# Late queries first in a fused attention and MLP kernel: the order of eight groups, the list's weights and its durations are changed

## The chip, the cores and the metric

The kernel runs on one core of a Trainium2 chip. The metric is device time in microseconds; the kernel before took 809.48 us (median of 3 runs, 809.31 to 809.81). The core's engines each have their own instruction stream: TensorE (PE) multiplies matrices and transposes, VectorE (DVE), ScalarE (ACT) and GpSimd (POOL) work on elements, and SyncE (SP) issues the transfers.

## The reference

```python
scores = (1 / np.sqrt(D)) * q @ k.T           # batch 4, heads 8, seq 576, head_dim 64
scores = np.where(block_i >= block_j, scores, -1e9)    # causal by blocks of 64
attn = softmax(scores) @ v                     # -> x: 2304 tokens x 512

h  = x @ w_in                                  # 512 -> 1024
s  = h * softmax(h)
x  = layernorm(s) * g_ln @ w_out               # 1024 -> 512

h  = x @ w2_in                                 # 512 -> 2048
out = (h * np.cos(h)) @ w2_out                 # 2048 -> 512
```

Three stages follow each other: attention, a first MLP with a layer norm, a second MLP with a cosine.

## The kernel before

Attention is cut into 32 pairs: 4 batches, 4 pairs of heads, and two sets of queries. Early queries are 0 to 255 of a sequence (they see at most 256 keys), late ones 256 to 575 (they see up to 576). A *group* is one batch with one set, so it holds four pairs; there are 8 groups. For each pair `trace_unit` makes score products of 128 queries (L495, the mask by small matmuls L498; the last 64 late queries in L530), the negated maximum (L506, L533 on DVE), the exponential with its sum (L509, L539 on ACT), the normalisation of `e` (L520, L522 or L524 on ACT, DVE or POOL; L551, L553, L555 for the last queries), and transposes of `e` (L581) that are copied to `eT` (L331 on ACT, L327 on DVE). `trace_pv` then multiplies by the values (L606) and leaves the result as high and low parts in `XS`, a ring of 640 tokens. An early pair has 6 transposes, a late one 19.

The groups fill 18 tiles of 128 tokens. When a tile is full, `trace_l1` multiplies it by w_in (L678, 6 matmuls per piece of weight: three products of high and low parts), takes the maximum (L682, DVE), the exponential (L683, ACT), h times softmax (L685, DVE) and the statistics (L694, ACT, and small ones); `trace_lnT` transposes the tile (L711), `trace_l2` multiplies by w_out (L732) and writes rows of yD. The second MLP runs after that (L771, the cosine L782 to L794, L811, L834).

The weights arrive as 64-bit numbers and are split in `trace_weight`: ACT does L635 and L636, DVE L637 and L639, POOL L641, and the high and low parts follow on whichever engine is chosen (L331, L327, L333; L336). w_in has 8 such pieces; the conversion runs while the first groups of attention run.

All this is an order written by a list scheduler at the time the kernel is built (`Scheduler.run`, L146 to L288). Each operation has a duration for every engine that may do it, a priority, and its dependencies. When an engine is free in the scheduler's model, it takes the ready operation with the lowest priority number, less an engine's offset; an operation that several engines can do goes to the one that would end it first by the durations times the `weight` of the engine. For PE an operation that changes the kind of work at a cost may be passed over for one that does not, within `stick`. Priorities come from a table `P` and from intervals per group (L842 to L859): `att_iv` gives each group a start and a length, 10000 ns for an early and 28600 for a late group plus 11000 per ready tile, and 25000 for the first group. The names in `P` shift these: `lead0` to `lead7` per group, `tile` per tile, `w_in` and `w_out` the weights. SP's transfers are ordered by the same list. Where the model has PE idle before 70 us, filler matmuls are put in (L953).

Of the kernel before, what the change touches and what calls it, by code (L numbers as in the profile page):

```python
# [28 lines left out]


P = {
    "stick": 16439.7,
    "tile": [-12965.7, -74277.3, -6661.5, 1158.2, 10885.7, -12920.0, 6417.0, -10505.1, -20606.0, 50938.7, -9661.6, 11449.5, 1147.6, 46246.4, -28708.3, -23619.0, -6397.2, -18072.8],
    "pair": [-2458.3, -5103.1, -897.3, 2369.0],
    "weight": {"p": 1.0, "s": 1.58, "v": 3.08, "g": 2.909, "q": 1.0},
    "att_slope": -0.012,
    "att_pe": 59777.9,
    "att_vec": 21108.6,
    "mlp_pe": -40513.6,
    "mlp_vec": 11906.3,  # L40
    "w_in": 4918.0,
    "w_out": 54908.8,
    "w_out_step": 3502.4,
    "w2_direct": -41386.8,
    "w2_step": 13014.7,
    "lead0": -7523.6,
    "lead1": 5369.7,
    "lead2": 14753.4,
    "lead3": 15930.2,
    "lead4": 14060.0,  # L50
    "lead5": -4515.5,
    "lead6": 10595.0,
    "lead7": -69178.6,
    "l2": 10939.5,
    "l2_step": 22673.5,
    "prep": -11366.2,
}


# [12 lines left out]
class Scheduler:  # L72
# [24 lines left out]
    def op(self, engs, fn, r=(), w=(), prio=0.0, port=False, iss=0.0, kind="M"):  # L97


        o = Op()  # L100
        o.engs, o.fn, o.prio, o.port, o.iss, o.kind = engs, fn, prio, port, iss, kind
        o.idx, o.succ, o.pred, o.ready, o.start = len(self.ops), [], [], {}, None
        deps, tiles = set(), []
        for k in list(r) + list(w):
            t = k[0] if isinstance(k, tuple) else k
            if isinstance(t, Lt) and t not in tiles:
                tiles.append(t)
        for k in r:
            if k in self.last_w:
                deps.add(self.last_w[k])  # L110
        for k in w:
            if k in self.last_w:
                deps.add(self.last_w[k])
            deps.update(self.reads.get(k, ()))
        for k in r:
            self.reads.setdefault(k, []).append(o)
        for k in w:
            self.last_w[k] = o
            self.reads[k] = []
        deps.discard(o)  # L120
        o.ndep = len(deps)
        for d in deps:
            d.succ.append(o)
        for t in tiles:
            t.refs += 1
        o.tiles = tiles
        self.ops.append(o)
        return o
# [163 lines left out]
def fused_kernel(ctx: ExitStack, tc: tile.TileContext, qT, kT, vm, vt, w_in, w_out, g_ln, w2_in, w2_out, out):  # L292
# [3 lines left out]
    NB = 4  # L296
# [5 lines left out]
    op = sch.op  # L302
# [115 lines left out]
    MLP = {"xs", "e1", "junk", "LN", "yb"}  # L418


    groups = [(b, g) for g in range(2) for b in range(NB)]
    gp_list = [(gi, p) for gi in range(len(groups)) for p in range(NPAIR)]

    def g_q0(gi):
# [5 lines left out]
    first, first_e = {}, {}  # L430
# [9 lines left out]
    def trace_prep(i, prio):  # L440
        gi, p = gp_list[i]
        b, g = groups[gi]
        pr = b * NPAIR + p
        nq, q0 = g_nq(gi), g_q0(gi)
        nk = q0 + nq
        nj = 2 if g == 0 else 4
        rv = Lt("rv", [128, 5, 2, 64], F32)
        rq, rk = Lt("rq", [128, nq], F32), Lt("rk", [128, nk], F32)
        dma(lambda: rq.ap, lambda: qT[pr, :, q0:q0 + nq], 512 * nq, w=[rq], prio=prio)
        dma(lambda: rk.ap, lambda: kT[pr, :, 0:nk], 512 * nk, w=[rk], prio=prio)  # L450
        dma(lambda: rv.ap[:, 0:nj], lambda: vm[pr, :, 0:nj, :].rearrange("p j (h d) -> p j h d", h=2), 65536 * nj,
            w=[(rv, 0)], prio=prio)
        if g == 1:
            dma(lambda: rv.ap[0:64, 4], lambda: vt[pr].rearrange("p (h d) -> p h d", h=2), 32768, w=[(rv, 1)], prio=prio)
        op({"s": c_s(nq), "v": c_v2(nq), "g": c_g(nq)}, lambda e: copy(e, rq.ap, rq.ap, SCALE), [], [rq], prio, port=True)
        return rq, rk, rv
# [4 lines left out]
    def trace_unit(i, t, prep, eT, prio):  # L461
        gi, p = gp_list[i]
        g = groups[gi][1]
        rq, rk, rv = prep
        q0 = g_q0(gi)
        W = 128 * (t + 1)
        us = Lt("us", [128, 8], F32)
        if g == 0:
            if t == 0:
                first_e[i] = [Lt("e", [128, 2, 128 * x + 128], F32) for x in range(2)]  # L470
            e = first_e[i][t]
        else:
            e = Lt("e", [128, 2, W] if t < 4 else [128, 640], F32)
# [3 lines left out]
        if row:  # L477
# [3 lines left out]
            scl = first[i]  # L481
            scs = [lambda h=h: scl[h].ap[:, 128 * t:128 * t + W] for h in range(2)]
            keys = [(x, t) for x in scl]
        else:
            scl = [Lt("psb", [128, W if t < 4 else 288], F32) for h in range(2)]
            scs = [lambda h=h: scl[h].ap for h in range(2)]
            keys = scl
        if t < 4:
            c0 = 128 * t - q0

            def f_s(spans):

                for n, (c, o, w) in enumerate(spans):
                    for h in range(2):
                        PE.matmul(scl[h].ap[:, o:o + w], lhsT=rq.ap[rows[h], c:c + 128], rhs=rk.ap[rows[h], 0:w], start=(n == 0), stop=False)  # L495
                for n, (c, o, w) in enumerate(spans):
                    for h in range(2):
                        PE.matmul(scl[h].ap[:, o + w - 64:o + w], lhsT=mrow[rows[h], :], rhs=mneg[rows[h], :],  # L498
                                  start=False, stop=(n == len(spans) - 1))
            if row and t == 0:  # L500
                op({"p": 790}, lambda _: f_s(((0, 0, 128), (128, 128, 256))), [rq, rk] + [(x, "a") for x in first_e[i]],
                   [(x, k) for x in scl for k in range(2)], prio, kind="W")
            elif not row:
                op({"p": W / 0.6 + 100}, lambda _: f_s(((c0, 0, W),)), [rq, rk, (e, "a")], scl, prio, kind="W")
            for h in range(2):
                op({"v": c_v(W)}, lambda _, h=h: V.tensor_reduce(out=us.ap[:, h:h + 1], in_=scs[h](), axis=AX.X, op=ALU.max, negate=True),  # L506
                   [keys[h]], [(us, h)], prio)
# [18 lines left out]
        else:  # L526
            for c in range(2):
                def f_s4(_, c=c):
                    for h in range(2):
                        PE.matmul(scl[c].ap[rows[h], :], lhsT=rq.ap[rows[h], 256:320], rhs=rk.ap[rows[h], 288 * c:288 * c + 288], start=True, stop=True)  # L530
                op({"p": 288 / 0.6 + 10}, f_s4, [rq, rk, (e, "a")], [scl[c]], prio, kind="W")
            for c in range(2):
                op({"v": c_v(288)}, lambda _, c=c: V.tensor_reduce(out=us.ap[:, c:c + 1], in_=scl[c].ap, axis=AX.X, op=ALU.max, negate=True),  # L533
                   [scl[c]], [(us, c)], prio)
# [311 lines left out]
    for gi in range(len(groups)):  # L846
        ready = [n for n in range(NT) if n >= done and tile_group[n] < gi]
        done += len(ready)
        ln = (10000.0 if groups[gi][1] == 0 else 28600.0) + T_TILE * len(ready)
        if gi == 0:  # L850
            ln = 25000.0
        att_iv.append((start, ln))
        for k, n in enumerate(ready):
            tile_pr[n] = start + ln * k / len(ready)
        start += ln
# [5 lines left out]
    for i, (gi, p) in enumerate(gp_list):  # L861
        us = (0, 1) if groups[gi][1] == 0 else (2, 3, 4)
        s_, l_ = att_iv[gi]
        pr = s_ + l_ * p / NPAIR - P[f"lead{gi}"] - P["pair"][p]
        prep = trace_prep(i, pr - P["prep"])
        n = 384 if groups[gi][1] == 0 else 1280
        eT = Lt("eT", [128, 2, n], F32)
        for k, t in enumerate(us):
            trace_unit(i, t, prep, eT, pr + l_ / NPAIR * k / len(us))
        trace_pv(i, prep, eT, pr + l_ / NPAIR)  # L870
# [8 lines left out]
    for n in range(NT):  # L879
        pr = tile_pr[n] + P["tile"][n]  # L880
        e = trace_l1(n, pr)
# [18 lines left out]
    for k in range(len(slots) + LAG):  # L900
        if k < len(slots):
            q, c, f = slots[k]
# [6 lines left out]
        if k >= LAG:  # L909
            q, c, f = slots[k - LAG]  # L910
# [20 lines left out]
    with tc.manual_schedule():  # L931
# [9 lines left out]
        for o in order:  # L941
            for t in o.tiles:
                if t.ap is None:
                    make, k, gate, _ = sch.classes[t.cls][t.slot]
# [4 lines left out]
            if o.idle is not None and o.start < WARM:  # L949

                b = singles[o.idle[1].slot] if o.idle[1].cls == "psb" else 2 * o.idle[1].slot
# [35 lines left out]
```

## Time and profile before

| | us |
| --- | --- |
| median of 3 runs | 809.48 |
| the profiled execution's own time | 808.07 |
| its span | 806.3 |
| PE busy in the span | 791.4 |
| DVE, ACT, POOL busy | 598.5, 479.2, 95.0 |

The profiled execution is one run; its span is the part that the trace shows. Busy time is time in which an engine has an instruction in work, and PE also counts as busy when it works slowly or runs fillers. The page's clock row is 9 (90% or more) in all forty slices; finer stretches are read from the rows below.

### The profile page before, as it was taken

How to read it: one execution, taken by the hardware profiler on the slowest of the kernel's cores; microseconds unless marked ns; L12 is line 12 of the kernel's file. 1: busy time of each engine (PE TensorE's matmuls, PEld its weight loads, DVE VectorE, ACT ScalarE, POOL GpSimd, SP SyncE). 2: the span in 40 equal slices, each digit the busy share in tenths (PEclk: the TensorE clock that was granted, in tenths of full speed). 3: DMA queues.
4: the chain of work that ended last, by engine and by line, in shares of the span. 5: the costliest groups of instructions: out<-in, count | busy, mean ns of one | idle time of the engine just before them, and what ended most of it. 6: DMA issues, size and time to landing. Idle time of an engine off the chain costs nothing.

```text
span 806.3 us, 12262 instructions
## 1 busy us (share of the span) xinstructions
PE 791.4 (98%) x4352; PEld 626.7 (78%) x4352; DVE 598.5 (74%) x1335; ACT 479.2 (59%) x1067; POOL 95.0 (12%) x116
## 2 busy tenths in 40 slices
PE   7989999999999999999999999999999999999998
PEld 5667766666776776788888888889988888888996
DVE  5889998667655367579978799866666676767775
ACT  6989998787765466668645667434434333333332
POOL 2222330000000000033322323100000000000000
PEclk9999999999999999999999999999999999999999
DMA  8443553222221101152535744121424022140221
GB/s 277 129 150 100 170 188 101 79 79 89 64 88 64 67 24 68 43 199 73 178 129 172 266 144 156 53 79 60 149 92 163 34 97 87 44 139 27 66 79 39
DMA packets 46029, 86.78 MB, mean 108 GB/s; under 512 B 4240, under 2 KB 18576, under 8 KB 45968
## 3 DMA queue, kind: packets, MB, share of 16 engines
q1 hardware_dynamic: 45968, 86.00, 32.1%
q8 instruction: 34, 0.56, 0.3%
q14 instruction: 27, 0.22, 0.1%
HBM read 67.11 MB, written 18.87 MB: 107 GB/s over the span
## 4 chain that ended last, share of the span: by engine, by line
PE 48%; DVE 1%; DMA 1%; ACT 0%; issue 0%
PE banks L811 24%; PE banks L771 23%; PE banks L732 1%; DMA rw<-w_in 1%; DVE w L336 0%; DVE t L639 0%; DVE ta L792 0%; ACT t L635 0%; DVE tr L787 0%; DVE rw L637 0%; DVE ob L834 0%; DVE LN L336 0%; ACT rw L636 0%; DVE YB L336 0%; ACT w L331 0%
## 5 line engine op out<-in xcount | busy, mean ns | idle before, releaser
L678 PE MATMUL banks<-w,XS 128*128 128x512 f32 x432 | 113.2, 404 | 1.5 <-DVE w L336 0.7
L331 ACT ACTIVATE gt<-ta 128x512 fp32r<-128x512 f32 (+1 forms) x80 | 47.1, 588 | 102.4 <-PE banks L811 69.8
L732 PE MATMUL banks<-LN,w 128*128 128x512 f32 (+1 forms) x480 | 105.6, 373 | 0.8 <-DVE LN L336 0.8
L732 PEld LDWEIGHTS banks<-LN,w 128*128 128x128 f32 x480 | 82.4, 189 | 17.7 <-DVE LN L336 1.2
L678 PEld LDWEIGHTS banks<-w,XS 128*128 128x128 f32 x432 | 77.3, 188 | 21.5 <-issue 4.7
L641 POOL TENSOR_TENSOR t<-t,rw 128x512 uint32<-128x512 uint32 x45 | 68.1, 1519 | 171.2 <-DVE t L639 86.6
L782 ACT ACTIVATE ta<-banks 128x512 f32<-128x512 f32 (+1 forms) x80 | 44.4, 555 | 73.9 <-PE banks L771 71.5
L783 DVE TENSOR_SCALAR ta<-ta 128x512 f32<-128x512 f32 (+1 forms) x80 | 37.0, 463 | 60.2 <-ACT ta L782 60.0
L811 PE MATMUL banks<-wa,gt 128*128 128x512 f32 x324 | 78.8, 390 | 0.0
L811 PE MATMUL banks<-w,gt 128*128 128x512 f32 x324 | 78.7, 390 | 0.0
L509 ACT ACTIVATE e<-banks,us 128x512 f32<-128x512 f32 (+3 forms) x128 | 66.5, 529 | 18.7 <-DVE us L506 17.9
L791 ACT ACTIVATE ta<-tr,hpi 128x512 f32<-128x512 f32 (+1 forms) x80 | 53.9, 674 | 29.0 <-DVE tr L789 28.7
L811 PEld LDWEIGHTS banks<-w,gt 128*128 128x128 f32 x324 | 60.6, 188 | 12.0
L811 PEld LDWEIGHTS banks<-wa,gt 128*128 128x128 f32 x324 | 60.6, 188 | 12.0
L506 DVE TENSOR_REDUCE us<-banks 128x1 f32<-128x512 f32 (+3 forms) x128 | 56.5, 482 | 15.1 <-PE banks L498 13.4
L336 DVE TENSOR_TENSOR gt<-ta,gt 128x512 fp32r<-128x512 f32 (+1 forms) x80 | 52.8, 661 | 14.9 <-ACT gt L331 14.0
L331 ACT ACTIVATE eT<-banks 128x512 f32<-128x512 f32 (+2 forms) x112 | 55.1, 531 | 11.8 <-PE banks L581 10.2
L581 PE MATMUL banks<-ident,e 128*128 128x128 f32 x400 | 58.2, 277 | 3.2 <-ACT e L520 1.8
L792 DVE TENSOR_TENSOR ta<-banks,ta 128x512 f32<-128x512 f32 (+1 forms) x80 | 50.9, 636 | 13.7 <-ACT ta L791 13.4
L581 PEld LDWEIGHTS banks<-ident,e 128*128 128x128 f32 x400 | 46.1, 141 | 16.3 <-ACT e L520 5.9
L606 PE MATMUL banks<-eT,rv 128*64 128x320 f32 (+3 forms) x448 | 53.3, 370 | 0.1
L787 DVE SCALAR_TENSOR_TENSOR tr<-ta,tr 128x512 f32<-128x512 f32 (+1 forms) x80 | 51.7, 646 | 2.2
(121 smaller groups left out, 1389.1 us busy)
## 6 DMA issues: line engine op xcount, KB each, us to landing
rw<-w_out SPq DMA_DIRECT2D x24, 512.0 KB, 4.0
rw<-w_in SPq DMA_DIRECT2D x22, 512.0 KB, 4.1
yD<-YB SPq DMA_DIRECT2D x16, 512.0 KB, 3.0
wa<-yD SPq DMA_DIRECT2D x7, 1024.0 KB, 6.4
rk<-kT SPq DMA_DIRECT2D x16, 288.0 KB, 2.9
oD<-ob SPq DMA_DIRECT2D x18, 256.0 KB, 2.4
w<-yD SPq DMA_DIRECT2D x6, 768.0 KB, 7.1
ob<-oD SPq DMA_DIRECT2D x18, 256.0 KB, 3.3
```

Of the source, the lines that this page charges most:

```text
L331: S.activation(dst, src, AF.Copy, scale=1.0 if scale is None else scale)
L336: (V if eng == "v" else G).tensor_tensor(out=dst, in0=src, in1=h.bitcast(F32), op=ALU.subtract)
L506: op({"v": c_v(W)}, lambda _, h=h: V.tensor_reduce(out=us.ap[:, h:h + 1], in_=scs[h](), axis=AX.X, op=ALU.max, negate=True), [keys[h]], [( ...
L509: op({"s": c_s(W, True, True)}, lambda _, h=h: S.activation(e.ap[:, h, :], scs[h](), AF.Exp, bias=us.ap[:, h:h + 1], scale=1.0, accum_out= ...
L581: PE.transpose(ps.ap[:, 128 * k:128 * k + 128], s(), ident)
L606: PE.matmul(pv.ap[64 * h:64 * h + 64, a:b], lhsT=rv.ap[0:rows, j, h], rhs=eT.ap[0:rows, h, c:c + b - a], start=(n == 0), stop=(n == len(se ...
L641: op({"g": c_g2(512)}, lambda _: G.tensor_tensor(out=t1.ap, in0=t1.ap, in1=lw(), op=ALU.add), [(rw, 0)], [t1], prio)
L678: PE.matmul(h.ap[:, 512 * c:512 * c + 512], lhsT=xs.ap[:, a, kt, :], rhs=w[:, b, 512 * c:512 * c + 512], start=(kt == 0 and a == 0 and b = ...
L732: PE.matmul(y.ap, lhsT=w[:, a], rhs=LN[:, b, kf, s0_:s0_ + len(t), :], start=(kf == 0 and a == 0 and b == 0), stop=(kf == 7 and b == 1))
L771: PE.matmul(ps.ap, lhsT=w[:, a, 128 * kt:128 * kt + 128], rhs=yts[q, c][kt // 2].ap[:, kt % 2, b, :], start=(k == 0), stop=(k == 11))
L791: op({"s": c_s(n, True)}, lambda _: S.activation(cs.ap, r.ap, AF.Sin, bias=hpi, scale=1.0), [r], [cs], prio)
L811: PE.matmul(acc[x][1](), lhsT=gt.ap[:, a, 128 * x:128 * x + 128], rhs=w[:, b, 512:1024], start=(f % 8 == 0 and k == 0), stop=(f % 8 == 7 a ...
```

## The change

The list of groups is turned around: `(1, 0)` puts the four groups of late queries first. Tokens in the ring and rows of yD follow that order. The table `P` has other numbers, among them the weights of ACT ("s", 1.58 to 2.385), DVE ("v", 3.08 to 2.75) and POOL ("g", 2.909 to 1.376). The durations of score products in the list become longer, and the first interval is 38000 when the first group is a late one.

```diff
 P = {
-    "weight": {"p": 1.0, "s": 1.58, "v": 3.08, "g": 2.909, "q": 1.0},
+    "weight": {"p": 1.0, "s": 2.385, "v": 2.75, "g": 1.376, "q": 1.0},
...
-    groups = [(b, g) for g in range(2) for b in range(NB)]
+    groups = [(b, g) for g in (1, 0) for b in range(NB)]
...
-                op({"p": 790}, lambda _: f_s(((0, 0, 128), (128, 128, 256))), [rq, rk] + [(x, "a") for x in first_e[i]],
+                op({"p": 900}, lambda _: f_s(((0, 0, 128), (128, 128, 256))), [rq, rk] + [(x, "a") for x in first_e[i]],
...
-                op({"p": W / 0.6 + 100}, lambda _: f_s(((c0, 0, W),)), [rq, rk, (e, "a")], scl, prio, kind="W")
+                op({"p": W / 0.6 + (120 if W == 384 else 190)}, lambda _: f_s(((c0, 0, W),)), [rq, rk, (e, "a")], scl, prio, kind="W")
...
-                op({"p": 288 / 0.6 + 10}, f_s4, [rq, rk, (e, "a")], [scl[c]], prio, kind="W")
+                op({"p": 288 / 0.6 + 70}, f_s4, [rq, rk, (e, "a")], [scl[c]], prio, kind="W")
...
-            ln = 25000.0
+            ln = 25000.0 if groups[0][1] == 0 else 38000.0
```

What that does to the order is seen on PE and POOL. A name such as `e_253` is one buffer of the program, and `x2` counts equal instructions that follow each other. On PE, at the end of the first wait for loads, the kernel before begins with the first early pairs, in scores of 128 and 256 keys:

```order
L495 MATMUL banks<-rk_109,rq_107 128x128 x2
L495 MATMUL banks<-rk_109,rq_107 128x256 x2
...
L581 MATMUL banks<-ident,e_124 128x128 x2
...
L581 MATMUL banks<-ident,e_125 128x128 x4
L495 MATMUL banks<-rk_120,rq_117 128x128 x2
...
L606 MATMUL banks<-eT_198,rv_111 64x256 x2
```

The changed one begins with two late pairs:

```order
L495 MATMUL banks<-rk_109,rq_107 128x384 x2
...
L495 MATMUL banks<-rk_109,rq_107 128x512 x2
...
L530 MATMUL banks<-rk_109,rq_107 64x288 x2
L495 MATMUL banks<-rk_116,rq_114 128x384 x2
...
L581 MATMUL banks<-ident,e_124 128x128 x3
```

The transposes behind the first scores now belong to a unit of 384 keys, and three tail score products of 288 keys stand where fillers stood. The second place is PE's first layer-1 matmul, L678. Before:

```order
L581 MATMUL banks<-ident,e_254 128x128 x4
L495 MATMUL banks<-rk_187,rq_184 128x128 x2
L495 MATMUL banks<-rk_187,rq_184 128x256 x2
...
L678 MATMUL banks<-w_287,XS 128x512 x6
L606 MATMUL banks<-eT_348,rv_122 64x256 x2
```

After:

```order
L606 MATMUL banks<-eT_422,rv_171 64x64 x2
L581 MATMUL banks<-ident,e_434 128x128 x3
L530 MATMUL banks<-rk_305,rq_302 64x288 x2
L581 MATMUL banks<-ident,e_459 128x128 x8
...
L581 MATMUL banks<-ident,e_468 128x128 x4
L678 MATMUL banks<-w_380,XS 128x512 x6
```

Before, it stands behind the scores of the fourth early pair; now the sixth late pair is under way. The third place is the start of POOL, after the masks are written. Before, it holds only sums of weights (L641):

```order
L938 MEMSET mhalf 128x1
L641 TENSOR_TENSOR t_196<-t_196,rw_113 128x512
L641 TENSOR_TENSOR t_249<-t_249,rw_115 128x512
L641 TENSOR_TENSOR YB<-YB,rw_168 128x512
L641 TENSOR_TENSOR YB<-YB,E_87 128x512
```

After, scalings of queries (L333), normalisations (L524) and parts of the split (L333, L336) stand among them:

```order
L938 MEMSET mhalf 128x1
L333 TENSOR_SCALAR rq_107<-rq_107 128x320
...
L524 TENSOR_SCALAR e_124<-e_124,us_179 128x384
...
L524 TENSOR_SCALAR e_196<-e_196,us_213 128x384 x2
...
L641 TENSOR_TENSOR t_267<-t_267,rw_182 128x512
...
L333 TENSOR_SCALAR w_380<-t_267 128x512
L336 TENSOR_TENSOR w_380<-t_267,w_380 128x512
```

Over the whole program POOL's normalisations (L524 and L555) go from 3 to 100, 30 of them of 384 columns and most of these in the late groups; fillers go from 112 to 51, and the places at which PE goes from one kind of work to another, fillers left out, from 242 to 218.

## Rows read from the trace of the kernel before

**Rows 1.** The page, busy time of each engine.

```profile
PE 791.4 (98%) x4352; PEld 626.7 (78%) x4352; DVE 598.5 (74%) x1335; ACT 479.2 (59%) x1067; POOL 95.0 (12%) x116
```

**Rows 2.** Busy by stretch: us, PE, PEld, DVE, ACT, POOL, clock, DMA share, GB/s.

```profile
5.30:59.50 54.20, 46.73 (x381) 33.61 (x379) 46.36 (x153) 48.01 (x150) 12.78 (x13) 0.97 0.59 191
59.50:112.20 52.70, 52.16 (x333) 38.93 (x332) 51.32 (x143) 50.10 (x138) 18.88 (x25) 1.00 0.43 136
112.20:344.40 232.20, 232.20 (x1453) 160.66 (x1453) 148.53 (x403) 161.56 (x398) 9.91 (x28) 1.00 0.25 78
```

**Rows 3.** Groups, 5.3 to 59.5 us; columns: busy us, mean ns, idle before.

```profile
L678 PE MATMUL banks<-w,XS 128*128 128x512 f32 x55 | 15.9, 416 | 1.5 <-DVE w L336 0.7 <-DVE w L327 0.5 <-DVE E L685 0.3
L581 PE MATMUL banks<-ident,e 128*128 128x128 f32 x54 | 9.8, 287 | 2.6 <-ACT e L520 1.3 <-DVE e L522 1.2
L495 PE MATMUL banks<-rk,rq 64*128 64x256 f32 x40 | 7.9, 410 | 0.0
L606 PE MATMUL banks<-eT,rv 128*64 128x256 f32 x36 | 6.3, 433 | 0.1
```

**Rows 4.** Timeline of PE, early pairs; columns: start us, us, operation.

```profile
24.55 0.87 PE L606 MATMUL banks<-eT,rv 128*64 128x256 f32 x8
25.35 0.93 PE L495 MATMUL banks<-rk,rq 64*128 64x128 f32 x8
...
26.26 1.66 PE L678 MATMUL banks<-w,XS 128*128 128x512 f32 x6
27.76 0.60 PE L581 MATMUL banks<-ident,e 128*128 128x128 f32 x4
```

**Rows 5.** Timeline of PE, late pairs and layer 1.

```profile
142.43 1.94 PE L581 MATMUL banks<-ident,e 128*128 128x128 f32 x16
144.30 2.42 PE L606 MATMUL banks<-eT,rv 128*64 128x320 f32 x20
146.66 0.92 PE L495 MATMUL banks<-rk,rq 64*128 64x384 f32 x4
...
344.36 7.11 PE L678 MATMUL banks<-w,XS 128*128 128x512 f32 x30
351.31 1.98 PE L732 MATMUL banks<-LN,w 128*128 128x512 f32 x8
```

**Rows 6.** Timeline of PE after a wait, and that stretch's busy times.

```profile
38.92 1.65 PE L495 MATMUL banks<-rk,rq 64*128 64x128 f32 x6 [0.80 <-ACT eT L331]
...
40.00:50.00 10.00, 9.14 (x58) 6.04 (x54) 7.72 (x26) 8.79 (x27) 2.59 (x2) 0.88 0.52 171
```

**Rows 7.** Groups of ACT, conversion of weights, whole span.

```profile
L636 ACT ACTIVATE rw<-rw 128x512 uint32<-128x512 uint32 x46 | 31.2, 678 | 3.9 <-DMA rw<-w_in 2.5 <-DMA rw<-w_out 1.3
...
L635 ACT ACTIVATE t<-rw 128x512 f32<-128x512 f32 x45 | 30.1, 672 | 5.1 <-DMA rw<-w_in 1.8 <-DVE w L336 1.5 <-DVE wa L336 0.7
```

**Rows 8.** Groups of a tile's chain behind layer 1.

```profile
L682 DVE TENSOR_REDUCE st<-banks 128x1 f32<-128x1024 f32 x18 | 21.9, 1218 | 10.0 <-PE banks L678 10.0
L685 DVE SCALAR_TENSOR_TENSOR E<-banks,E 128x1024 f32<-128x1024 f32 x18 | 21.9, 1216 | 1.4 <-ACT E L683 1.3
...
L694 ACT ACTIVATE junk<-E,st 128x1024 bf16<-128x1024 f32 x18 | 20.7, 1149 | 3.2 <-DVE st L687 3.2
L683 ACT ACTIVATE E<-banks,st 128x1024 f32<-128x1024 f32 x18 | 20.2, 1123 | 4.6 <-DVE st L682 4.5
```

**Rows 9.** DMA issues: KB each, median us to landing.

```profile
rk<-kT SPq DMA_DIRECT2D x16, 288.0 KB, 2.9
...
rk<-kT SPq DMA_DIRECT2D x16, 128.0 KB, 2.5
```

**Rows 10.** Normalisation on POOL and DVE (group, ns min/median/max), with DVE beside it.

```profile
L524 POOL TENSOR_SCALAR e<-e,us x3: 374/376/943, 59.0 to 68.7; 128x128 f32<-128x128 f32 x3
...
59.40 0.74 DVE L647 SCALAR_TENSOR_TENSOR w<-t,g_sb,w 128x512 fp32r<-128x512 f32 x1
...
L522 DVE TENSOR_SCALAR e<-e,us 128x384 f32<-128x384 f32 x15 | 6.1, 418 | 0.4
```

More of the change, by code (lines that the diff above doesn't have):

```diff
@@ L31 @@
 P = {
-    "stick": 16439.7,
-    "tile": [-12965.7, -74277.3, -6661.5, 1158.2, 10885.7, -12920.0, 6417.0, -10505.1, -20606.0, 50938.7, -9661.6, 11449.5, 1147.6, 46246.4, -28708.3, -23619.0, -6397.2, -18072.8],
-    "pair": [-2458.3, -5103.1, -897.3, 2369.0],
-    "weight": {"p": 1.0, "s": 1.58, "v": 3.08, "g": 2.909, "q": 1.0},
[L36 to L56, printed above, removed]
+    "stick": 24783.0,
+    "tile": [-14359.3, -37985.7, 6113.4, -3055.7, 24465.2, 4623.7, 3526.9, -32896.1, -22525.7, 27230.1, -18199.6, 22478.0, 37632.5, 59648.4, -15097.6, 596.8, -22562.3, -32058.0],
+    "pair": [-10908.6, 3875.9, 1648.0, 792.0],
+    "weight": {"p": 1.0, "s": 2.385, "v": 2.75, "g": 1.376, "q": 1.0},
+    "att_slope": 0.053,
+    "att_pe": 74866.7,
+    "att_vec": 151894.2,
+    "mlp_pe": -14159.9,
+    "mlp_vec": 34158.7,
+    "w_in": -10429.3,
+    "w_out": 307495.7,
+    "w_out_step": 1138.4,
+    "w2_direct": 73027.9,
+    "w2_step": 12920.1,
+    "lead0": 7512.5,
+    "lead1": 22625.7,
+    "lead2": 8969.7,
+    "lead3": -7974.6,
+    "lead4": -9446.8,
+    "lead5": -67400.4,
+    "lead6": -7144.6,
+    "lead7": -13408.6,
+    "l2": 5241.5,
+    "l2_step": 15170.5,
+    "prep": 36287.5,
 }
```

## The prediction

> **What bounds the kernel now.** I began with the page: TensorE (PE) is busy for 791.4 of 806.3 us [rows 1]. By that figure 14.9 us could be won at most, but it also counts the filler matmuls of L953, slowed matmuls and matmuls whose tail merely waits, so I went on to the busy time by stretch [rows 2]. Two stretches show PE full: from 59.5 to 344.4 us it idles 0.54 and 0.00 us. The stretch 5.3 to 59.5, in which the early pairs run beside the conversion of w_in and the first tiles of layer 1, is different: PE 46.73 of 54.20, ACT 48.01, DVE 46.36, PE's clock 0.97. No engine is full; three are nearly full and take turns.
>
> Next I asked what PE computes there. The costliest groups [rows 3] give 55 L678 (9 groups of 6), 54 transposes L581, 40 wide score matmuls (4 in each of 10 score operations) and 36 wide L606 (4 in each of 9 value products). The timeline [rows 4] prices each from start to start where PE does not wait: a value product 25.35 − 24.55 = 0.80; a score operation with its masks 26.26 − 25.35 = 0.91; six L678 27.76 − 26.26 = 1.50; a transpose (144.30 − 142.43)/16 = 0.117 [rows 5]. So the stretch needs 9×0.80 + 10×0.91 + 54×0.117 + 9×1.50 = 7.2 + 9.1 + 6.3 + 13.5 = 36.1 us. It takes 54.2, and 18.1 us are lost. ACT alone accounts for 48.0 − 36.1 = 11.9 of them, as it has 48.0 us to do beside 36.1 of PE; the other 6.2 are hand-offs, in which ACT too is idle. Part of the loss shows as busy time: between 40 and 50 the clock is 0.88, and there six score matmuls took 1.65 where eight take 0.93 [rows 4, 6], after a PE wait of 0.80 for ACT.
>
> In 112.2 to 344.4, where mostly late pairs run, ACT is busy for 161.56 and DVE for 148.53 of 232.20 [rows 2], that is 70% and 64%. Late pairs keep PE full and leave ACT and DVE time.
>
> **The change part by part.** PE computes the same matmuls. What moves is which pairs stand beside the weight conversions.
>
> *Late pairs in the first stretch.* One late pair gives PE 19 transposes at 0.117, 2.2 us, value products of 146.66 − 144.30 = 2.36 [rows 5], and three rounds of score products, each at no less than the early 0.91: at least 7.3 us. In the new order some five pairs' worth stands before the first L678, 36.5 us. ACT needs 0.70 × 36.5 = 25.5 for them. Converting w_in's 8 pieces takes ACT 8 × (0.672 + 0.678) = 10.8 [rows 7]. Together 36.3: ACT's need falls from 11.9 above PE's to none. The hand-offs remain in kind, but each is now followed by pieces of three to eight transposes (0.35 to 0.94) or a 2.36 us product rather than by two to four transposes or 0.80; I keep 70% of the 6.2. Left of the 18.1: 4.3. Bounds: 2 (a third of the hand-offs) and 18.1 (nothing won).
>
> *Early pairs later.* They still want more of ACT than PE takes, but there they stand among layer-1 and layer-2 matmuls of tiles already finished, with w_in and w_out converted. That cover can run out at the turn from late to early groups, where a tile's layer 1 in the new order ends some 7 us of PE work before its next step. The chain that must fit between is L682 1.218, L683 1.123, L685 1.216, L694 1.149 [rows 8], 4.7 us before hand-offs. If three of them and some short operations use the same engines for others meanwhile, it does not fit. Bounds 0 and 12 (ACT's whole excess, met again); I take 1.0, as the stretch 59.5 to 112.2 does much the same with an idle of 0.54 [rows 2].
>
> *First loads.* Keys come as 288 KB in 2.9 us where 128 KB took 2.5 [rows 9]; the first scores are later by 0.4, and a scaling of 320 columns for 256 makes it 0.5. Nothing covers it. Bounds 0.4 and 1.
>
> *Changes of kind on PE.* The order has 24 fewer places at which PE goes from one kind of work to another (218 for 242, fillers aside). Six L678 cost 1.50 from start to start, thirty 351.31 − 344.36 = 6.95 [rows 4, 5]; from 1.50 = a + 6b and 6.95 = a + 30b, one beginning costs a = 0.14. 24 of them are 3.3 us; transposes and value products show less, so I take −2.0. Bounds 0 and −3.3.
>
> *POOL.* Normalisations on POOL (L524, L555) go from 3 to 100, 30 of them 128x384. ACT and DVE are relieved by them; on PE's path they can cost. A pass of 384 on DVE takes 0.418; on POOL only 128 columns are shown, at 0.374, 0.376 and 0.943, the last beside L647 on DVE from 59.40 [rows 10]. So a 384 pass lies between 0.42 (as DVE) and 3 × 0.374 + 0.57 of waiting = 1.69. While PE has other pairs' transposes and products to do, 1.2 us are hidden, and I count 0. If that cover is gone it is up to 1.27 each; the rival below prices it.
>
> *Score durations, fillers, phase 2.* The durations and the first interval only steer the list: 0 by themselves. Fillers fall from 112 to 51; they run when PE would wait, so 0. MLP2 and the tail keep their rows: 0, with no bound other than 0.5 either way.
>
> Sum, against the profiled execution: 806.3 − 18.1 + 4.3 + 1.0 + 0.5 − 2.0 = 792.0 us of span. Its own time lies 808.07 − 806.3 = 1.77 above its span: 793.8. The median of the runs, 809.48, lies 1.41 above that execution: **795.2 us**. The best ends (2, 0, 0.4, −3.3) give 787.3 of span, 790.5.
>
> **Rivals.** *Half the gain.* PE still waits for ACT at the start, since maxima, exponentials and copies of late pairs come in a chain before any other pair is ready, and the turn costs 3 us. With 9.0 of 18.1 left, 3.0, 0.5 and −1.5: 799.2 of span, 802.4 us. For it: DVE is at 46.36 in the stretch now and a late pair brings 64% of its PE time besides. Against: ACT's two conversions are the bigger part and do fit.
>
> *No change.* The 18.1 us belong to the ramp itself, whichever pairs come first: all of it left gives 806.3 + 1.0 + 0.5 − 2.0 = 805.8, or 809.0 us. [...] Against: the two rates of ACT to PE, 48.0 to 36.1 and 161.6 to 232.2.
>
> *POOL on PE's path: slower.* The first 30 passes of 384 sit in the stretch where only two or three pairs are open; each pass delays that half pair's transposes. At 1.2 us, near the upper end since the L524 row with DVE beside it shows the wait, 18 of 30 exposed cost 21.6 us: 817 us. It turns from faster to slower by over 0.2% at (811.1 − 795.2)/1.2 = 13 passes. For it: 0.943 against 0.374. Against: in the new first stretch PE has other work in reach, and ACT and DVE lose just these passes. The row, then, shows a POOL pass that took two and a half times as long with a DVE instruction beside it. The Trainium skill, "SBUF — State Buffer", Who interferes with whom, has the two engines share one pair of ports as an exclusive lock, the loser fully blocked; "Perfetto Trace Analysis", Optimizing Scalar/DVE Operations, adds that moving work between those two might not help. By that rule the lock would also hold up DVE's two-operand passes, and the 817 us would be the likely case rather than a rival; the trace agrees on the one wait, and does not show how often it happens.
>
> **How the numbers follow.** The forecast (788 to 800) has 0.62; half the gain (800 to 807.9) 0.22; no change (within 0.2% of 809.48, 807.9 to 811.1, about what a measurement of this kernel can tell from none) 0.05; POOL, and any slower outcome, 0.11. Hence faster 0.84, same 0.05, slower 0.11. The range 787 to 807 leaves out the last two and the edges: its lower end is 3.5 below the best sum because my start-to-start prices may still hold short waits, its upper end takes in nearly all of the half gain.
>
> **What would show it.** Right: in the first 60 us PE's idle and fillers fall, ACT is no longer the engine that most of PE's waits name; after 60 us PE idles no more than 3 us up to phase 2. Half gain: PE's waits in the first stretch name ACT or DVE and sum to over 5 us, or an idle stretch stands at the late-to-early turn. POOL: L581 waits for e from L524, which takes over 1 us. Wrong altogether: the clock stays under 0.9 for a stretch, or phase 2 changes its length.

## The result and the profile after

The changed kernel takes 796.94 us (median of 4 runs, 796.31 to 797.87) where the kernel before took 809.39 in the same comparison: a ratio of 0.9849, 95% interval 0.9832 to 0.9866, so 1.5% faster. The forecast was 795.2, with 787 to 807 as its range.

The profiled execution's own time is 796.97 us, its span 795.2 against 806.3, 11.1 less. First the page's busy times, then the busy time by stretch (columns as in [rows 2]; TensorE's first score product starts at 5.9, before at 5.3):

```profile
PE 784.4 (99%) x4291; PEld 622.1 (78%) x4291; DVE 588.0 (74%) x1238; ACT 421.8 (53%) x944; POOL 219.2 (28%) x320
```

```profile
5.90:59.50 53.60, 52.38 (x369) 31.26 (x367) 48.19 (x126) 47.24 (x128) 32.40 (x45) 1.00 0.56 181
59.50:112.20 52.70, 52.70 (x366) 32.96 (x366) 49.73 (x119) 46.12 (x113) 28.42 (x43) 1.00 0.45 141
112.20:344.40 232.20, 231.21 (x1423) 174.84 (x1420) 145.16 (x386) 136.27 (x370) 81.89 (x156) 1.00 0.29 93
402.80:470.00 67.20, 64.31 (x280) 52.01 (x279) 62.10 (x95) 35.63 (x62) 29.40 (x24) 1.00 0.52 179
```

The first row answers to the first of [rows 2]: TensorE (PE) idles 1.2 us there, not 7.5, and its clock is 1.00, not 0.97. ACT and DVE are as busy as they were; what they serve is more. POOL has 32 us of work there instead of 13. New losses stand in the last two rows, 1.0 and 2.9 us of idle.

How much work PE got done in the first stretch is read from its groups (busy us, mean ns, idle before), with prices from the timeline below them (start, duration), as the prediction did it:

```profile
L581 PE MATMUL banks<-ident,e 128*128 128x128 f32 x120 | 17.2, 280 | 0.4 <-POOL e L524 0.4
L495 PE MATMUL banks<-rk,rq 64*128 64x512 f32 x28 | 8.1, 639 | 0.0
L530 PE MATMUL banks<-rk,rq 64*64 64x288 f32 x48 | 7.8, 422 | 0.2 <-ACT e L509 0.2
L606 PE MATMUL banks<-eT,rv 128*64 128x320 f32 x48 | 7.3, 441 | 0.0
L678 PE MATMUL banks<-w,XS 128*128 128x512 f32 x24 | 6.6, 409 | 0.0
L495 PE MATMUL banks<-rk,rq 64*128 64x384 f32 x28 | 6.4, 532 | 0.6 <-POOL us L513 0.6
...
L606 PE MATMUL banks<-eT,rv 128*64 128x192 f32 x16 | 2.0, 326 | 0.0
L606 PE MATMUL banks<-eT,rv 64*64 64x64 f32 x16 | 1.3, 243 | 0.0
```

```profile
41.95 0.70 PE L530 MATMUL banks<-rk,rq 64*64 64x288 f32 x4
42.58 0.92 PE L495 MATMUL banks<-rk,rq 64*128 64x384 f32 x4
...
43.45 2.42 PE L606 MATMUL banks<-eT,rv 128*64 128x320 f32 x20
45.81 1.42 PE L581 MATMUL banks<-ident,e 128*128 128x128 f32 x11
47.16 1.13 PE L495 MATMUL banks<-rk,rq 64*128 64x512 f32 x4
...
48.25 1.00 PE L581 MATMUL banks<-ident,e 128*128 128x128 f32 x6
```

From start to start, four L530 take 0.63, four L495 of 384 with their masks 0.87, four of 512 1.09, a value product of 20 L606 2.36. With 0.117 per transpose and 1.50 for six L678 [rows 4, 5] the stretch holds 120 × 0.117 + 7 × 1.09 + 12 × 0.63 + 4 × 2.36 + 4 × 1.50 + 7 × 0.87 = 14.0 + 7.6 + 7.6 + 9.4 + 6.0 + 6.1 = 50.7 us of work in 53.6. The loss is 2.9 us. Counted the same way, matmul by matmul from the first score, it was 17.8 before. One late pair is 2.2 + 2.36 + 0.87 + 1.09 + 2 × 0.63 = 7.8 us of PE's work by these prices.

Not all of ACT's room comes from the late pairs. The kernel before also converts the first pieces of w_out in this stretch, loaded from 38.5 us on; the changed one loads the first of them at 58.1. ACT's two passes per piece (L635, then L636) in the stretch, before, changed, and with the order alone (an experiment below):

```profile
5.30:59.50 54.20, 6.70 (x10) 0.97 0.59 191
5.30:59.50 54.20, 7.47 (x11) 0.97 0.59 191
...
5.30:59.50 54.20, 4.82 (x7) 1.00 0.56 180
5.30:59.50 54.20, 5.54 (x8) 1.00 0.56 180
...
5.30:59.50 54.20, 5.49 (x8) 1.00 0.56 184
5.30:59.50 54.20, 5.55 (x8) 1.00 0.56 184
```

That is 14.2 us before and 10.4 after: 3.8 us of ACT's work left the stretch because the list now places it later. Without the conversions ACT has 48.0 − 14.2 = 33.8 us beside 36.4 of PE's work before, 0.93 us for each, and 47.2 − 10.4 = 36.9 beside 50.7 after, 0.73.

PE's waits over the whole span (us in total, times, longest) show what is left:

```profile
PE banks L771 <- DVE ta L792: 2.9, 4, 1.4
PE banks L953 <- POOL mrow L936: 2.0, 1, 2.0
PE banks L581 <- POOL e L524: 0.7, 3, 0.4
PE banks L495 <- POOL us L513: 0.6, 1, 0.6
```

The longest is no longer in attention: PE's first matmuls of the second MLP wait for the cosine. Four rows of the timeline show the longest of these waits; the fifth is the cosine step L787 of 512 columns in the kernel before (48 passes, 33.8 us, 705 ns each):

```profile
418.43 1.63 POOL L641 TENSOR_TENSOR t<-t,rw 128x512 uint32<-128x512 uint32 x1 [1.61 <-ACT gt L331]
418.82 1.79 DVE L787 SCALAR_TENSOR_TENSOR tr<-ta,tr 128x512 f32<-128x512 f32 x1
...
422.75 0.69 DVE L792 TENSOR_TENSOR ta<-banks,ta 128x512 f32<-128x512 f32 x1 [0.79 <-ACT ta L791]
...
423.59 1.16 PE L771 MATMUL banks<-wa,w 128*128 128x512 f32 x4 [1.38 <-DVE ta L792]
...
L787 DVE SCALAR_TENSOR_TENSOR tr<-ta,tr 128x512 f32<-128x512 f32 x48 | 33.8, 705 | 1.1
```

DVE's cosine step L787 takes 1.79 us, 1.09 more than the 0.705. POOL's L641 runs from 418.43 to 420.06, so the two overlap for 1.24 us, and L787 ends at 420.61, 0.55 us behind POOL. It stood still for nearly all of the overlap. The Trainium skill, "SBUF — State Buffer", Who interferes with whom, says of the two engines' shared ports that they are an exclusive lock, the loser fully blocked. The trace agrees here but for some 0.15 us. L641 stands on POOL in the kernel before too; what is new on POOL beside the second MLP are L333 and L336, and an experiment below takes them away.

The 11.1 us then add up as follows. First stretch: 17.8 − 2.9 = 14.9 gained. Later first score: 0.6 lost. Waits behind DVE at the start of the second MLP: 2.9 in 402.8 to 470 us, against 1.17 of the kernel before (0.37 before an L711 and 0.80 before an L732 of the first MLP's last tile), 1.7 lost. The turn to early groups, 250 to 310 us: 58.6 us of work by the same prices in 60 (L711 as a transpose, L732 at 0.227, the prediction's price of a matmul without its beginning), where the kernel before had 61.7 (matmuls of one kind in a row cost less than their price, hence more than 60): 3.1 lost. Only 0.8 of that is idle time of PE. Counted in the two traces, PE goes 49 times from one kind of work to another in these 60 us and 31 times before; at the prediction's 0.14 each, 18 more are 2.5 us, an estimate that with the 0.8 comes to about the 3.1. Gains and losses together make 9.5; the other 1.6 are spread over the rest, where fewer changes of kind were counted on; no run measures them by themselves.

### The profile page after: what moved, and what is told of

The parts are those of the page before. It is cut to its first block, busy times and chain, and to the rows that moved or that the text cites. A ratio compares the mean times of both kernels' runs of the same rounds, so it can differ in the third digit from the quotient of the medians.

```text
span 795.2 us, 12231 instructions
## 1 busy us (share of the span) xinstructions
PE 784.4 (99%) x4291; PEld 622.1 (78%) x4291; DVE 588.0 (74%) x1238; ACT 421.8 (53%) x944; POOL 219.2 (28%) x320
## 4 chain that ended last, share of the span: by engine, by line
PE 86%; DVE 4%; DMA 3%; ACT 2%; POOL 2%; issue 1%; SPq 0%; ACTq 0%; POOLq 0%
PE banks L771 22%; PE banks L811 22%; PE banks L732 13%; PE banks L678 11%; PE banks L606 6%; PE banks L581 5%; PE banks L495 4%; DMA rq<-qT 3%; PE banks L530 2%; PE banks L711 2%; POOL e L524 1%; DVE tr L787 1%; DVE gt L336 1%; DMA rw<-w_out 1%; POOL t L641 0%
## 5 line engine op out<-in xcount | busy, mean ns | idle before, releaser
L678 PE MATMUL banks<-w,XS 128*128 128x512 f32 x432 | 110.5, 401 | 0.0
L732 PE MATMUL banks<-LN,w 128*128 128x512 f32 (+1 forms) x480 | 103.8, 372 | 0.0
L732 PEld LDWEIGHTS banks<-LN,w 128*128 128x128 f32 x480 | 83.1, 189 | 15.1 <-DVE LN L336 0.2
L678 PEld LDWEIGHTS banks<-w,XS 128*128 128x128 f32 x432 | 78.0, 188 | 18.6 <-issue 3.4
L811 PE MATMUL banks<-w,gt 128*128 128x512 f32 x378 | 91.8, 390 | 0.0
L641 POOL TENSOR_TENSOR t<-t,rw 128x512 uint32<-128x512 uint32 x45 | 63.8, 1419 | 80.3 <-DVE t L639 21.4
L811 PEld LDWEIGHTS banks<-w,gt 128*128 128x128 f32 x378 | 70.8, 188 | 14.1
L509 ACT ACTIVATE e<-banks,us 128x384 f32<-128x384 f32 (+3 forms) x128 | 66.3, 530 | 20.0 <-DVE us L506 18.0
L506 DVE TENSOR_REDUCE us<-banks 128x1 f32<-128x384 f32 (+3 forms) x128 | 56.0, 481 | 14.8 <-PE banks L498 11.0
L336 DVE TENSOR_TENSOR gt<-ta,gt 128x512 fp32r<-128x512 f32 (+1 forms) x80 | 54.0, 675 | 16.4 <-ACT gt L331 15.6
L811 PE MATMUL banks<-wa,gt 128*128 128x512 f32 x270 | 65.7, 390 | 0.0
L524 POOL TENSOR_SCALAR e<-e,us 128x384 f32<-128x384 f32 (+3 forms) x97 | 49.1, 518 | 37.8 <-ACT e L509 20.4
L331 ACT ACTIVATE eT<-banks 128x512 f32<-128x512 f32 (+3 forms) x104 | 50.4, 525 | 16.0 <-PE banks L581 15.3
L811 PEld LDWEIGHTS banks<-wa,gt 128*128 128x128 f32 x270 | 50.5, 188 | 10.1
L787 DVE SCALAR_TENSOR_TENSOR tr<-ta,tr 128x512 f32<-128x512 f32 (+1 forms) x80 | 55.3, 692 | 2.2
```

The costliest lines, as they stand in the source:

```text
L331: S.activation(dst, src, AF.Copy, scale=1.0 if scale is None else scale)
L336: (V if eng == "v" else G).tensor_tensor(out=dst, in0=src, in1=h.bitcast(F32), op=ALU.subtract)
L509: op({"s": c_s(W, True, True)}, lambda _, h=h: S.activation(e.ap[:, h, :], scs[h](), AF.Exp, bias=us.ap[:, h:h + 1], scale=1.0, accum_out= ...
L524: G.tensor_scalar(out=a, in0=a, scalar1=us.ap[:, 6 + h:7 + h], scalar2=1.0, op0=ALU.mult, op1=ALU.mult)
L641: op({"g": c_g2(512)}, lambda _: G.tensor_tensor(out=t1.ap, in0=t1.ap, in1=lw(), op=ALU.add), [(rw, 0)], [t1], prio)
L678: PE.matmul(h.ap[:, 512 * c:512 * c + 512], lhsT=xs.ap[:, a, kt, :], rhs=w[:, b, 512 * c:512 * c + 512], start=(kt == 0 and a == 0 and b = ...
```

## The experiments

Two sorts of edit have to be kept apart. One leaves the list as it is and changes an instruction when it is written out: every other instruction keeps its place. The other changes what the list is planned from, and everything after the first difference is placed anew. How much that alone can do is told second. Each experiment was timed beside the kernel before on one chip (its medians there 808.54 to 809.46), so it is the ratios that compare.

**The order of the groups alone.** The kernel before with `groups` turned around and the first interval of 38000:

```diff
-    groups = [(b, g) for g in range(2) for b in range(NB)]
+    groups = [(b, g) for g in (1, 0) for b in range(NB)]
...
-            ln = 25000.0
+            ln = 25000.0 if groups[0][1] == 0 else 38000.0
```

> The kernel before with nothing changed but the order of the groups (late first) and the first interval of 38000; the table, the engines' weights and the durations are those of before, POOL keeps 5 normalisations. Theory A (late pairs need less of ACT per us of TensorE work, so w_in's conversion fits beside them): most of the gain is here, 797 to 802 us, and the first 60 us have under 6 us of waits and fillers on TensorE. Rival B (the gain is the new engine weights, that is POOL's 100 normalisations): 806 us or more. Rival C (only table and order tuned to each other gain): 803 to 812.

Measured: 839.89 us, ratio 1.0394 (1.0367 to 1.0422). Theories A and C are off by over 25 us; rival B's "806 or more" is met, though not for its reason (the weights with the new durations, below, gain nothing). Its windows and waits:

```profile
5.90:59.50 53.60, 46.72 (x350) 27.14 (x348) 42.82 (x120) 50.21 (x125) 10.05 (x9) 1.00 0.55 183
70.00:80.00 10.00, 6.59 (x27) 4.65 (x27) 8.55 (x22) 7.11 (x16) 3.64 (x4) 0.69 0.31 101
```

```profile
PE banks L678 <- DVE E L685: 10.1, 8, 3.4
PE banks L732 <- DVE ta L792: 6.0, 1, 6.0
```

By the prices above the first stretch loses 11.7 us, so the order by itself takes 6.1 of the 17.8 away there, with ACT at 50.21 of 53.60. Without the conversions that is 50.2 − 11.0 = 39.2 us of ACT beside 41.8 of PE's work, 0.94: with the old weights the new stretch asks as much of ACT per us of PE's work as the old one did. The rest of the span loses more than was won: tiles' chains behind layer 1 come too late for PE, for 10.1 us in eight waits. In 70 to 80 us, which hold one of 3.4, the granted clock is 0.69, a mean of its two levels, 1.2 and 2.4 GHz.

**Ten nanoseconds.** The changed kernel with each score duration 10 longer:

```diff
-                op({"p": 900}, ...
+                op({"p": 910}, ...
...
-                op({"p": W / 0.6 + (120 if W == 384 else 190)}, ...
+                op({"p": W / 0.6 + (130 if W == 384 else 200)}, ...
...
-                op({"p": 288 / 0.6 + 70}, ...
+                op({"p": 288 / 0.6 + 80}, ...
```

> The changed kernel with each score duration 10 ns longer (910, 130 or 200, 80): an edit that no trace would ask for, to see how much any new order of the list moves the time. If the 9 us of the old durations come of the list being wrong about TensorE: 795 to 799 us. If any replanning loses several us because the table is fitted to one order: 800 to 808, and then e5, e6 and e10 carry that much uncertainty in what they say of their edit.

Measured: 814.9 us, 1.0075 of the kernel before (1.0053 to 1.0096), some 18 us more than the changed kernel and above both expected ranges. PE's waits, and the stretches in which it loses:

```profile
PE banks L771 <- DVE ta L792: 3.6, 4, 2.3
PE banks L581 <- POOL e L524: 3.2, 5, 1.1
...
PE banks L678 <- ACT e L509: 1.7, 1, 1.7
PE banks L678 <- DVE E L685: 1.3, 1, 1.3
```

```profile
112.20:344.40 232.20, 225.23 (x1379) 166.56 (x1378) 138.04 (x367) 127.66 (x356) 73.86 (x156) 0.99 0.27 84
```

Its first stretch loses 5.0 us. Most of the 18 is lost later: from 112.2 to 344.4 PE idles 7.0 us, not 1.0. So the time of a replanned kernel says little of its edit; what happens in one stretch, and in every order that has the edit, says more.

**The old durations**, put back in the changed kernel:

```diff
-                op({"p": 900}, ...
+                op({"p": 790}, ...
...
-                op({"p": W / 0.6 + (120 if W == 384 else 190)}, ...
+                op({"p": W / 0.6 + 100}, ...
...
-                op({"p": 288 / 0.6 + 70}, ...
+                op({"p": 288 / 0.6 + 10}, ...
```

> The changed kernel with the score durations of before (790, W/0.6+100, 288/0.6+10), so that the list thinks TensorE faster by 20 to 110 ns per score product. If the durations only steer the list and matter little: within 3 us of the changed kernel, 794 to 800. If the table is fitted to them as closely as to the order: 802 or more.

Measured: 806.34 us, 0.9959 (0.9944 to 0.9974), 9 us of the gain gone; 5.2 lost in the first stretch, and the longest waits of PE are

```profile
PE banks L771 <- DVE ta L792: 3.8, 4, 2.5
PE banks L581 <- POOL e L524: 3.0, 5, 1.1
```

By its own terms this would say that the table is fitted to the durations; beside the ten nanoseconds it says that it is fitted to this one plan.

**The weights with the durations, and the weights taken back.** The kernel before with ACT 2.385, DVE 2.75, POOL 1.376 and the new durations, early groups first:

```diff
-    "weight": {"p": 1.0, "s": 1.58, "v": 3.08, "g": 2.909, "q": 1.0},
+    "weight": {"p": 1.0, "s": 2.385, "v": 2.75, "g": 1.376, "q": 1.0},
...
```

> The kernel before, early groups first, with the changed weights of ACT, DVE and POOL and the changed score durations alone; POOL gets 97 normalisations. Theory A: no gain, 806 to 814 us, since the first stretch still has early pairs beside w_in's conversion; ACT's busy time there falls but hand-offs grow. Rival B (POOL's relief of ACT and DVE is the gain): 796 to 802.

Measured: 819.70 us, ratio 1.0138 (1.0118 to 1.0158), above theory A's range and far from rival B's. The first stretch loses 21.0, though ACT and DVE are relieved by 33 passes on POOL:

```profile
5.90:59.50 53.60, 46.41 (x435) 35.44 (x436) 36.94 (x114) 38.26 (x121) 39.40 (x60) 0.97 0.56 178
```

ACT is busy for 38.26 us there, about 10 less than before, and nothing is won. In this order no engine is nearly full; what is lost goes into waits of one engine for the next. The reverse edit in the changed kernel, its durations kept:

```diff
-    "weight": {"p": 1.0, "s": 2.385, "v": 2.75, "g": 1.376, "q": 1.0},
+    "weight": {"p": 1.0, "s": 1.58, "v": 3.08, "g": 2.909, "q": 1.0},
```

> The changed kernel with the engines' weights of before (ACT 1.58, DVE 3.08, POOL 2.909); POOL then gets 3 normalisations instead of 100. Theory E (order and POOL's relief of ACT are both needed in the first stretch, where ACT is busy 95% of the time in 10 to 40 us): 6 to 11 us lost there instead of 2.8, 800 to 806 us. Theory A alone (late pairs first suffice once tiles and groups have fitting priorities): 795 to 799.

Measured: 811.47 us, 1.0027 (1.0015 to 1.0039): above theory E's range, with a loss of 8.9 in the first stretch that lies within it. As single plans, the weights are worth 14.5 us with the late pairs first (811.47 to 796.94) and, with the durations, cost some 10 with the early ones first. This run also differs from the order alone by the other priorities of `P` and the durations; the two are 28 us apart (839.89 to 811.47). No run tries those priorities by themselves, so what share of the gain is theirs stays open.

**POOL struck from the normalisation.** In the changed kernel:

```diff
-                op({"s": c_s(W, True), "v": c_v2(W) + 65, "g": c_g(W, True)}, f_n, ...
+                op({"s": c_s(W, True), "v": c_v2(W) + 65}, f_n, ...
```

and likewise for the last queries.

> The changed kernel, its weights kept, with POOL struck from the engines that may normalise (L524, L555): all 128 units go to ACT and DVE, the query scalings and weight parts stay on POOL. Theory E: 13 normalisations of 0.6 us come back to ACT and DVE in the first stretch; 3 to 7 us slower than the changed kernel, 800 to 804. Theory A alone: within 2 us of it.

Measured: 803.53 us, 0.9932 (0.9911 to 0.9954), as theory E has it. The first stretch loses 7.1, and the engine that is full there is now DVE, 51.30 of 53.60:

```profile
5.90:59.50 53.60, 50.02 (x357) 29.17 (x355) 51.30 (x134) 45.38 (x122) 21.60 (x30) 1.00 0.57 187
```

The first stretch of all these orders, from the first score to 59.5 us: passes in the stretch, and us lost:

| kernel | first groups | L524 and L555 | L635 and L636 | lost |
| --- | --- | --- | --- | --- |
| before | early | 2 | 21 | 17.8 |
| weights and durations | early | 33 | 21 | 21.0 |
| order alone | late | 0 | 16 | 11.7 |
| changed, old weights | late | 0 | 19 | 8.9 |
| changed, POOL struck | late | 0 | 17 | 7.1 |
| changed, old durations | late | 17 | 15 | 5.2 |
| changed, ten ns more | late | 18 | 15 | 5.0 |
| changed | late | 14 | 15 | 2.9 |

Each order with late pairs first loses less than each with early ones, and of the late ones each with POOL's passes less than each without. Passes on POOL gained nothing in the one order with early pairs first that has them. These are eight orders and not eight repetitions of two, so the sizes are rough; the sign of both is the same in all of them. But the late orders without POOL's passes also convert more in the stretch, by one to four passes of ACT of 0.68 us, up to 2.7 us. That is less than the differences in loss, yet it is a part of them; no run moves POOL's passes back in a fixed order.

**ACT's work doubled in one pass.** In either kernel's own order, the first pass over each of w_in's 8 pieces is written twice:

```diff
-        op({"s": c_s(512)}, lambda _: S.activation(f1(), hw(), AF.Copy, scale=F64_SCALE), [rw], [t1], prio)
+        twice = any(w8 is x for x in w_in_t)
+        op({"s": c_s(512)}, lambda _: [S.activation(f1(), hw(), AF.Copy, scale=F64_SCALE) for _ in range(1 + twice)], [rw], [t1], prio)
```

> The kernel before in its order, with ACT's pass L635 done twice for each of w_in's 8 pieces (the same values written twice): 8 x 0.672 = 5.4 us more of ACT's work, all in the first stretch. Theory A (ACT's need sets that stretch's length): 4 to 5.4 us slower than before, 813 to 815. Rival D (hand-offs or DVE set it, ACT has room): at most 2 us slower, 809 to 811.5.

Measured: 814.18 us, 1.0073 (1.0053 to 1.0092), 5.6 more than the 808.54 of before beside it. Time added to ACT there is time added to the whole, as theory A has it. The run does not tell ACT's need from the chain of hand-offs in which this pass stands; no run lengthens a pass of DVE in the same way.

> The changed kernel in its order with the same doubled pass, 5.4 us more of ACT's work in the first stretch. There ACT is busy 47.2 of 53.6 us. Theory A (ACT no longer sets the length): at most 2 us slower than the changed kernel, 797 to 799. If ACT still sets it: 4 to 5.4 us slower, 801 to 802.5.

Measured: 801.50 us, 0.9915 (0.9900 to 0.9931), 4.6 more than the changed kernel's 796.94 (by the ratios 0.9915 − 0.9849, 5.3). My expectation was wrong. The tenths of the stretch tell why; first the changed kernel, then this one:

```profile
10.00:20.00 10.00, 9.79 (x82) 5.75 (x78) 9.47 (x32) 9.33 (x28) 2.82 (x7) 1.00 0.98 353
20.00:30.00 10.00, 9.64 (x72) 5.83 (x70) 9.56 (x21) 9.62 (x27) 6.03 (x10) 1.00 0.55 173
30.00:40.00 10.00, 10.00 (x75) 5.30 (x72) 9.34 (x25) 9.53 (x25) 7.12 (x10) 1.00 0.42 134
```

```profile
10.00:20.00 10.00, 9.25 (x76) 5.39 (x74) 9.19 (x30) 9.93 (x31) 2.90 (x7) 1.00 0.98 355
20.00:30.00 10.00, 9.54 (x73) 5.46 (x69) 8.97 (x22) 9.90 (x26) 6.11 (x10) 1.00 0.51 164
30.00:40.00 10.00, 8.72 (x60) 4.33 (x60) 8.06 (x22) 9.94 (x27) 6.28 (x8) 1.00 0.40 119
```

I had taken ACT's room from the mean, 47.2 of 53.6 us. But in 10 to 40 us, where the conversion is, ACT was already busy 28.5 of 30, DVE 28.4 and PE 29.4: all nearly full at once. With the longer pass ACT is full (29.8), DVE falls to 26.2 and PE idles 2.5 of 30. So ACT was not freed; its need and PE's were made equal.

**POOL beside the second MLP.** In the changed kernel's order, the high parts of weights other than w_in's that stand on POOL (L333) are written for ACT:

```diff
-            op_hi(512, d[0], f1, [t1], [(w8, part, 0)], prio)
+            op({"s": c_s(512), "v": c_v2(512), "g": c_g(512)}, lambda e: copy("s" if e == "g" and not any(w8 is x for x in w_in_t) else e, d[0](), f1()), [t1], [(w8, part, 0)], prio, port=True)
```

> The changed kernel in its order, but the high parts of all weights but w_in that POOL made (L333 beside phase 2) made by ACT at the same place. Theory F (DVE's cosine steps stand still behind POOL passes in 400 to 470 us, so that TensorE waits 2.9 us for ta): half to all of the waits go, 794 to 796 us. Rival G (DVE has too much to do there anyway, or L641 alone blocks it): within 1 us of the changed kernel.

Measured: 795.35 us, 0.9828 (0.9809 to 0.9848), within theory F's range, though its interval overlaps the changed kernel's. The waits for ta go from 2.9 to 1.4 us: half, and the rest is not L333's. With nine low parts (L336) on DVE as well:

```diff
-            op_lo(512, d[1], f1, d[0], [t1, (w8, part, 0)], [(w8, part, 1)], prio)
+            op({"v": c_v(512), "g": c_g2(512)}, lambda e: sub("v" if not any(w8 is x for x in w_in_t) else e, d[1](), f1(), d[0]()), [t1, (w8, part, 0)], [(w8, part, 1)], prio, port=True)
```

> As e7, and the low parts of the same weights (L336, 10 passes of 1.3 to 1.8 us on POOL) on DVE, at 0.66 each. Theory F: POOL keeps only L641 beside phase 2 as in the kernel before, the waits for ta fall from 1.4 us to under 1, 793.5 to 795.5 us. Rival: DVE is too full there (62 of 67 us busy in 402.8 to 470), and these passes delay the cosine: 796 or more.

Measured: 794.83 us (794.49 to 795.07), 0.9814 (0.9798 to 0.9830), an interval that lies just below the changed kernel's 0.9849 (0.9832 to 0.9866). The waits for ta are 1.2 us, not under 1. The rows of 402.8 to 470, PE 65.99 where it was 64.31, ACT 42.65 where it was 35.63, and its waits:

```profile
402.80:470.00 67.20, 65.99 (x290) 53.96 (x289) 59.69 (x102) 42.65 (x74) 16.59 (x12) 1.00 0.51 180
```

```profile
PE banks L771 <- DVE ta L792: 1.2, 2, 0.7
PE banks L581 <- POOL e L524: 0.9, 2, 0.7
```

DVE is busy for less time although it does more: 59.69 against 62.10. Time in which it stood still behind POOL counted as busy. Both waits that are left come behind an L787 of 1.80 us beside L641, at 418.92 and at 458.09. This version beats both kernels, the changed one by 0.3%.

**Normalisation at the turn.** At the turn PE's transposes follow POOL pass by pass:

```profile
268.76 1.63 POOL L524 TENSOR_SCALAR e<-e,us 128x128 f32<-128x128 f32 x4
...
269.28 1.04 PE L581 MATMUL banks<-ident,e 128*128 128x128 f32 x3
```

The second head's passes of early pairs, where on POOL, are put on DVE in the same order:

```diff
                 def f_n(q, h=h):
+                    if q == "g" and g == 0 and h == 1:
+                        q = "v"
```

> The changed kernel in its order, with the second head's normalisation of the early pairs that POOL made (31 to 62 passes of 128 and 256 columns) on DVE instead. Theory H (at the turn, 260 to 305 us, TensorE waits for passes that stand in line on POOL): the loss there falls from some 3 us to 1, 794 to 796 us. Rival: the chain through ACT's exponentials is late itself, or DVE's queue is held up: no change or slower, 797 to 800.

Measured: 796.57 us, 0.9845 (0.9827 to 0.9863): between the two expected ranges, and no difference to the changed kernel that can be told. The loss of 250 to 310 us goes from 1.4 to 0.8 by prices, but PE's idle time there from 0.8 to 1.0, so theory H is not borne out. With the two edits of the last part (high parts on ACT, low parts on DVE) added to it:

> e9 with e8's normalisation on DVE as well. Sum of the measured effects: 0.4 us less than e9, which is within what can be told apart; 793 to 795.5 us. If DVE becomes late at the turn: above e9.

Measured: 796.08 us, 0.9829 (0.9813 to 0.9846), above its range and 1.25 us above the version without it. At the turn POOL's line is not what costs: most of the 3.1 us is no wait at all, but more changes of kind, as far as the estimate above goes.

## Why the prediction was right

The total came out within 2 us, and the loss fell where it was said to fall: in the first stretch PE's idle time goes from 7.5 to 1.2 us and its fillers from 80 to 13, no wait of PE there over 0.2 us names ACT any more, and from 59.5 to 402.8 us PE idles 1.0 us, within the 3 that were allowed. Term by term, where the span was to be 792.0 and is 795.2:

- *Loss left in the first stretch:* 4.3 expected, 2.9 measured. That the conversions fit beside late pairs is borne out: ACT's need then equals PE's (25.5 + 10.8 beside 36.5, expected; 28.5 beside 29.4 of 30, measured). The doubled pass costs about its full length in both kernels, so ACT's time still counts after the change; it came to par with PE's, not below.
- *But the order was not enough.* The step "ACT's need falls ... to none" took 0.70 us of ACT per us of PE for late pairs from a stretch in which half of PE's time is the first MLP's (L678 53.2, L711 10.1 and L732 56.7 of 232.2 us), and let the order alone bring it. With the order alone it was 0.94; in the changed kernel, with the new weights and POOL's passes, it is 0.73. In the six late-first orders of the table the three without POOL's passes lose 7.1 to 11.7 and the three with them 2.9 to 5.2. The prediction counted POOL at 0, as neither gain nor cost; by the table it was part of the gain. Nor did it speak of the 3.8 us of ACT's conversions that went out of the stretch, which are part of the gain there too.
- *Turn:* 1.0 expected within 0 to 12, 3.1 measured by prices, of which 0.8 is idle time. Its place was right; that the chain L682 to L694 is its cause was not shown for the changed kernel. In the order-alone kernel that chain cost 10.1 us, in waits from 75 to 397 us.
- *First loads:* 0.5 expected, 0.6 measured. *Changes of kind:* −2.0 expected; −1.6 is what remains unexplained, which fits but is not a measurement of it.
- *Second MLP:* "0, with no bound other than 0.5 either way" was wrong: 1.7 us. I had followed POOL's new work only to the normalisations, and not to L333 and L336 beside the cosine, although the lock between POOL and DVE was named in the rival.
- *Durations:* "0 by themselves" cannot be kept. They choose the plan, and plans differ by up to 18 us at ten nanoseconds.
- *From execution to median:* I added 1.41, the distance of that one execution from its median. After, the two agree within 0.03.

Part of the close number is luck. The span missed by 3.2 us, and nearly half of that was cancelled by the 1.41 that did not come. And the prediction reasoned from the order, while the same order with the old table and weights takes 839.89 us: that this table would let the rest of the span keep the gain was assumed, not derived.

The rival in which POOL's passes stand on PE's path did not come: 384 columns took 0.665 us on POOL (30 passes), between the bounds of 0.42 and 1.69, and PE waited 0.7 us for e in all:

```profile
L524 POOL TENSOR_SCALAR e<-e,us 128x384 f32<-128x384 f32 x30 | 19.7, 665 | 10.8 <-DVE us L515 9.2 <-ACT eT L331 0.8 <-DVE us L535 0.7
```

In two replanned orders, the old durations and ten nanoseconds, it came in part, at 3.0 and 3.2 us where the rival had 21.6. The rival "half the gain" had the turn at 3 us about right and the first stretch wrong.

## What to carry to other kernels

Where no engine is full but three are nearly so, count what each needs in that stretch per us of the bounding engine's work, and put work with a different ratio there; take an engine's room from the part where the extra work stands, not from the mean of the stretch. A change to a list's inputs is a new plan, and its time is the plan's: test parts in a fixed order, or compare one stretch over several plans. Work given to POOL must be followed to every place where DVE runs beside it.

## What the runs showed of the hardware that was not expected

- DVE can stand still for nearly the whole overlap with a POOL pass and shows it as busy time: L787 took 1.79 us beside L641, 1.24 of them in overlap, against a mean of 0.705 for 512 columns in the kernel before. With L333 and L336 taken off POOL in 402.8 to 470 us, DVE's busy time fell by 2.4 us, although three of the passes had come to it.
- In the order-alone kernel PE's granted clock was 0.69 in the ten us around a wait of 3.4; in the changed kernel, with no wait over 0.7 between its first score and 59.5 us, it is 1.00 over that stretch, where the kernel before had 0.88 in 40 to 50 us, after a wait of 0.80 [rows 6]. After another wait of 0.80, before an L732 at 411.7 us, the kernel before kept 1.00 (402.8 to 470).
